# q by tokens for dK: from a scratch tensor in DRAM to replicated copies and transposes inside SBUF

## The chip, the cores and the metric

The kernel runs on one core of one Trainium2 chip. A core has five engines that run independent instruction streams in order and wait for one another on semaphores: TensorE (PE, with weight loads shown apart as PEld), VectorE (DVE), ScalarE (ACT), GpSimd (POOL) and SyncE (SP). Transfers are issued by SP, ACT or POOL and carried out by 16 DMA engines. The metric is the device time of one execution in microseconds; less is better.

## The reference

Two attention blocks stand side by side, and the kernel computes the forward output and all gradients for a given gradient of the output. A is a linear attention; it comes first in time and the change does not touch it. B is an attention with 16 query heads of 28 columns over one shared head of keys and values, for 2048 tokens:

```python
q = (x @ wq).reshape(B, S, H, Dh).transpose(0, 2, 1, 3)   # 16 heads
k = x @ wk                                                # one head
v = x @ wv
scores = einsum("bhqd,bkd->bhqk", q, k) * Dh ** -0.5
p = softmax(scores)
o = einsum("bhqk,bkd->bhqd", p, v)
out = o.transpose(0, 2, 1, 3).reshape(B, S, H * Dh) @ wo
```

For the gradients, with dS the gradient of the scores, dQ is dS times k, and dK is the sum over all heads and queries of dS transposed times q. For dK, q is needed with tokens on the partitions ("q by tokens"), while the scores need it with columns on the partitions (R1, also called qT_B). How q by tokens is made is what changes.

## The kernel before

Block A runs first, then the projections of block B (phase_B_pre): keys, values and q are computed with columns on the partitions; R1 holds four groups g of 128 rows (4 heads of 32 padded columns), 2048 tokens long. q_shift computes a softmax offset for each query and put_shift writes it by small DMAs into row 0 of each head in R1.

The core of block B is one loop over steps u (512 steps and 28 more to drain). A block b of 8 steps is one pair of heads by 256 queries; a step is 256 keys. Eight blocks (64 steps) share a chunk qc of 256 queries. The order of the work is written out by hand (manual_schedule), and the stages are shifted against each other by fixed lags:

- step u: PE makes the scores (rows_SD); ACT turns their two halves into eT by exp (L914, L964).
- w = u - 16: PE makes dP in two banks DB; DVE multiplies the first half with eT into dsT (L925); ACT copies the second half to cp (L927), and POOL multiplies it (L928). dsT has 5 buffers (pool pd_), cp has 3.
- u - 18: DVE transposes dsT in 32 by 32 blocks into dsx (L995), at the end of its step, and so needs both halves.
- u - 20 and u - 19, at even steps: PE sums dQ from dsT (dq_mm).
- u - 27, at odd steps: PE sums dK from dsx and qX (dk_m, L834).
- every fourth step (u % 4 == 3) SP issues a DMA transpose of 32 tiles of 128x128, eT to eN (L966), which dV uses 13 steps later and more (dv_mm). It is the main work of SP's queue.
- once a block POOL also computes prod, don and an R2 entry (o_norm, L808 to L812) and one small product (L817).

Before the change q by tokens comes to qX so. For the first 1024 tokens, phase_B_pre transposes R1 by DMA into qn (L598) and stores it to the DRAM tensor qn_d (L599). For the others, four DMA transposes ahead of the loop fill a second qn (L893), which POOL stores to qn_d in four parts at steps 34 to 58 (L930). POOL then loads each chunk from qn_d in four parts of 32 partitions (L937): at steps 10 to 22 chunk 0, at 66 to 78 chunk 1, and at steps 34, 42, 50 and 58 of each later 64 the next chunk. A buffer qX is [128, 4, 2, 512]: token (b, j, s) stands on partition j of each of four groups of 32 partitions, since the four row groups of the PE each need q. wo, the output weight, is loaded by POOL at step 86, and the softmax offsets of token groups 2 and 3 are put by POOL at step 1.

The DMA issues of POOL are POOL's own instructions: they stand in its stream and take its time. SP's stand in SP's queue[...].

## Time and profile before

| what | before |
|---|---|
| time, median of 3 runs (lowest, highest) | 1080.56 us (1078.34, 1083.28) |
| the profiled execution's own time | 1082.27 us |
| its span, first to last instruction | 1080.6 us |
| busy: PE, DVE, ACT, POOL | 95%, 83%, 81%, 72% |
| TensorE clock, mean over the span | 0.994 |
| first and last exp of the loop (L914) start at | 218.5 and 1003.6 us |
| steps 16 to 34, by the start of their exp | 237.9 to 278.7 us |
| a block of 8 steps later on | 11.96 to 12.17 us for most |

The page of a profile lists the engines' busy time, groups of instructions by line of the kernel with their number and mean time, and a chain: the work that ended last, followed back through what released each step. A trace can also be listed in order of time. "PE agen L661" in a wait is an engine, what it writes and the line; "SPq" is SP's queue. Line numbers are those of the kernel before.

### The profile page before, as it was taken

How to read it: one execution, taken by the hardware profiler on the slowest of the kernel's cores; microseconds unless marked ns; L12 is line 12 of the kernel's file. 1: busy time of each engine (PE TensorE's matmuls, PEld its weight loads, DVE VectorE, ACT ScalarE, POOL GpSimd, SP SyncE). 2: the span in 40 equal slices, each digit the busy share in tenths (PEclk: the TensorE clock that was granted, in tenths of full speed). 3: DMA queues.
4: the chain of work that ended last, by engine and by line, in shares of the span. 5: the costliest groups of instructions: out<-in, count | busy, mean ns of one | idle time of the engine just before them, and what ended most of it. 6: DMA issues, size and time to landing. Idle time of an engine off the chain costs nothing.

```text
span 1080.6 us, 39970 instructions
## 1 busy us (share of the span) xinstructions
PE 1026.0 (95%) x16241; PEld 484.7 (45%) x16241; DVE 898.0 (83%) x1793; ACT 873.2 (81%) x1741; POOL 774.0 (72%) x1018
## 2 busy tenths in 40 slices
PE   9999999996999999999999999999999999999998
PEld 5555545432444444444444444444444444444434
DVE  7887400556999999999999999999999999999933
ACT  6463122585999999999999999999999999999622
POOL 6001242235899888888988988988988898888881
PEclk9999999997999999999999999999999999999999
DMA  9759899199999999999999999999999999999973
GB/s 265 160 110 199 173 204 228 30 185 151 204 208 211 203 202 188 200 180 210 179 185 197 196 195 187 203 181 188 185 209 187 196 198 162 206 187 181 223 133 90
DMA packets 668305, 199.34 MB, mean 184 GB/s; under 512 B 646056, under 2 KB 663760, under 8 KB 668120
## 3 DMA queue, kind: packets, MB, share of 16 engines
q1 hardware_dynamic: 655256, 174.18, 95.7%
q0 software_dynamic: 7904, 18.64, 6.8%
q10 hardware_dynamic: 4960, 3.96, 1.3%
q8 instruction: 127, 2.08, 0.8%
q14 instruction: 58, 0.48, 0.1%
HBM read 20.99 MB, written 12.94 MB: 31 GB/s over the span
## 4 chain that ended last, share of the span: by engine, by line
PE 37%; POOL 21%; ACT 18%; DVE 11%; issue 10%; DMA 4%; ACTq 0%; DVEq 0%; POOLq 0%
POOL dsT L928 16%; PE agen L82 14%; ACT cp L927 9%; ACT eT L964 7%; PE agen L661 7%; PE aacc L82 7%; PE aacc L661 6%; DVE dsx L995 4%; DVE dsT L925 2%; DMA eN<-eT 2%; POOL prod L808 2%; POOL don L811 1%; POOL R L812 1%; ACT eT L914 1%; DMA qX<-qn_d 1%
## 5 line engine op out<-in xcount | busy, mean ns | idle before, releaser
L928 POOL TENSOR_TENSOR dsT<-cp,eT 128x512 bf16<-128x512 bf16 x512 | 587.8, 1156 | 103.7 <-ACT cp L927 97.2
L995 DVE STREAM_TRANSPOSE dsx<-dsT 128x512 f32<-128x512 f32 x512 | 358.0, 699 | 2.8 <-POOL dsT L928 0.3
L925 DVE TENSOR_TENSOR dsT<-agen,eT 128x512 bf16<-128x512 f32 x512 | 342.1, 668 | 20.0 <-PE agen L661 15.2
L661 PEld LDWEIGHTS <-R 32*128 32x128 bf16 (+1 forms) x9104 | 225.3, 94 | 276.1 <-issue 239.5
L914 ACT ACTIVATE eT<-aacc 128x512 bf16<-128x512 f32 x512 | 313.2, 612 | 26.7 <-PE agen L661 15.8
L927 ACT ACTIVATE cp<-agen 128x512 bf16<-128x512 f32 x512 | 315.4, 616 | 12.3 <-PE agen L661 11.2
L964 ACT ACTIVATE eT<-aacc 128x512 bf16<-128x512 f32 x512 | 321.7, 628 | 0.0
L661 PE MATMUL agen<-dsx,qX 32*32 32x512 bf16 x4096 | 269.0, 376 | 3.5 <-DMA qX<-qn_d 3.5
L661 PE MATMUL agen<-doT,R 32*128 32x256 bf16 x2048 | 248.1, 270 | 3.3 <-DVE dsT L925 1.6
L661 PE MATMUL aacc<-R,R 32*128 32x256 bf16 (+1 forms) x2240 | 218.8, 269 | 5.8 <-DVE oTs L804 1.3
L661 PE MATMUL agen<-eT,R 128*32 128x256 bf16 x2048 | 158.2, 275 | 0.1
L661 PE MATMUL agen<-dsT,R 128*32 128x256 bf16 x2048 | 157.3, 275 | 0.1
L661 PEld LDWEIGHTS <-qX 32*32 32x32 bf16 x4096 | 80.1, 89 | 118.4 <-issue 54.6
L661 PE MATMUL aacc<-eN,don 128*32 128x512 bf16 x1024 | 98.1, 383 | 4.3 <-DMA eN<-eT 4.3
L82 PEld LDWEIGHTS <-R 128*128 128x128 bf16 (+1 forms) x517 | 41.0, 99 | 43.9 <-issue 12.3
L407 POOL COPY pk<-R 128x256 bf16<-128x256 bf16 x4 | 1.6, 397 | 73.8 <-DVE R L367 73.7
L82 PE MATMUL agen<-R,R 128*128 128x448 bf16 (+1 forms) x180 | 42.9, 366 | 0.5 <-ACT R L226 0.5
L661 PEld LDWEIGHTS <-don 128*32 128x32 bf16 x1024 | 33.9, 98 | 5.3 <-issue 4.7
L423 DVE TENSOR_TENSOR osb<-aacc,pr 64x448 bf16<-64x448 f32 x2 | 1.2, 617 | 39.1 <-DMA out_dram<-osb 24.9
L825 PE MATMUL aacc<-identB,don 128*32 128x128 bf16 x256 | 18.6, 224 | 14.0 <-POOL don L817 10.2
L949 DVE TENSOR_SCALAR R<-agen 64x256 bf16<-64x256 f32 x64 | 27.3, 427 | 3.6 <-PE agen L661 1.6
L517 ACT ACTIVATE wdq<-agen 128x448 bf16<-128x448 f32 x16 | 8.7, 543 | 24.7 <-PE agen L82 24.7
(232 smaller groups left out, 987.7 us busy)
## 6 DMA issues: line engine op xcount, KB each, us to landing
qX<-qn_d POOLq DMA_DIRECT2D x32, 256.0 KB, 4.4
out_dram<-osb ACTq DMA_DIRECT2D x22, 112.0 KB
eN<-eT SPq DMA_TRANSPOSE x128
xa<-in_A_x_dram SPq DMA_DIRECT2D x8, 224.0 KB
ga<-in_grad_out_dram SPq DMA_DIRECT2D x4, 448.0 KB
xa<-in_grad_out_dram POOLq DMA_DIRECT2D x4, 448.0 KB, 5.8
out_dram<-wdq POOLq DMA_DIRECT2D x8, 224.0 KB, 4.9
eT<-in_grad_out_dram SPq DMA_DIRECT2D x4, 448.0 KB
```

The source lines that it names most:

```text
L82: nc.tensor.matmul(out_ap, lhsT=lhsT, rhs=rhs, start=start, stop=stop, tile_position=(0, 0))
L661: nc.tensor.matmul(out, lhsT=lhsT, rhs=rhs, start=start, stop=stop, tile_position=pos, skip_group_check=True)
L808: nc.gpsimd.tensor_tensor(out=prod[b][:], in0=dnv, in1=os_, op=ALU.mult)
L811: nc.gpsimd.tensor_tensor(out=dn[:], in0=dnv, in1=r_[:].to_broadcast([P, 2, 2, 32]), op=ALU.mult)
L825: nc.tensor.transpose(tp2[q:q + 32, qb * P:(qb + 1) * P], don[b][:, qb, h, :], identB[:, :], tile_position=(0, q))
L914: nc.scalar.activation(out=eT(u)[:, 0, :], in_=sp[0][:, :], func=ACT.Exp, scale=scale)
L925: nc.vector.tensor_tensor(out=dst[:, 0, :], in0=dp[0][:, :], in1=ew[:, 0, :], op=ALU.mult)
L927: nc.scalar.activation(out=cp[:, :], in_=dp[1][:, :], func=ACT.Copy)
L928: nc.gpsimd.tensor_tensor(out=dst[:, 1, :], in0=cp[:, :], in1=ew[:, 1, :], op=ALU.mult)
L949: nc.vector.tensor_scalar(out=qT_B[g][64 * hp:64 * hp + 64, qc * 256:(qc + 1) * 256], in0=oq[64:128, 0:256], scalar1=scale, scalar2=None, ...
L964: nc.scalar.activation(out=eT(u)[:, 1, :], in_=sp[1][:, :], func=ACT.Exp, scale=scale)
L995: nc.vector.transpose(out=dsx[b][:, tp, :, :, :].rearrange("p h t c -> p (h t c)").bitcast(F32), in_=dsT[y][:, :, :].rearrange("p h c -> p ...
```

## The change

The scratch tensor qn_d is gone. For each chunk and group g the columns of R1 are copied inside SBUF into a staging tile, each token repeated four times (qc_copy, two instructions, one per parity s of the token), and one DMA transpose of 8 tiles (qc_T) turns that into the 128 columns g of qX, so that the four partition groups receive their copies at once. Chunk 0 is made ahead of the loop, half of the copies on POOL and half on VectorE, through four of the dsT buffers. The later chunks use one staging tile, qst (a single buffer); POOL copies at steps 30 + 8g and 32 + 8g of each 64, and SP's transpose is issued at step 35 + 8g, behind the eN transpose of the same step. The buffers of even and odd chunks change places. wo is loaded by SP ahead of the loop, and the offsets of token groups 2 and 3 are put by SP at step 11. Everything of PE and ACT stays in its order.

```diff
-            if qc == 1:
-                for g in range(4):
-                    nc.sync.dma_start_transpose(qn[:, :, g * P:(g + 1) * P], qT[:, g, 0:1024])
-                nc.sync.dma_start(qn_d[0:1024, :].rearrange("(t p) c -> p t c", p=P), qn)
...
+        qst = pp_.tile([P, 8, 4, 32], BF16, name="qst", bufs=1)[:, :, :, :]
...
+        def qc_copy(eng, st, qc, g, s):
+            src = qT_B[g][:, qc * 256:(qc + 1) * 256].rearrange("p (b j s) -> p b j s", b=4, s=2)[:, :, :, s]
+            eng.tensor_copy(out=st.rearrange("p (b s) a j -> p b s a j", s=2)[:, :, s, :, :],
+                            in_=src.unsqueeze(2).to_broadcast([P, 4, 4, 32]))
+
+        def qc_T(st, qc, g):
+            nc.sync.dma_start_transpose(qX[qc].rearrange("p b s c -> p (b s) c")[:, :, g * P:(g + 1) * P],
+                                        st.rearrange("p n a j -> p (n a j)"))
...
-            qn = pqa_.tile([P, 8, 512], BF16, name="qX")
+            nc.sync.dma_start(wo, wo_d[:, 0:D].rearrange("(g p) c -> p g c", p=P))
+            qX[0] = pqa_.tile([P, 4, 2, 512], BF16, name="qX")
             for g in range(4):
-                nc.sync.dma_start_transpose(qn[:, :, g * P:(g + 1) * P], R1[:, g, 1024:2048])
+                st = pd_.tile([P, 2, 512], BF16, name="dsT").rearrange("p a (n j) -> p a n j", j=32).rearrange(
+                    "p a (n b) j -> p (a n) b j", b=4)
+                qc_copy(nc.gpsimd, st, 0, g, 0)
+                qc_copy(nc.vector, st, 0, g, 1)
+                qc_T(st, 0, g)
...
-                    for qc in (2, 3):
-                        put_shift(shifts[qc], slice(qc * 512, qc * 512 + 512))
...
+                if u == 11:
+                    for n in (2, 3):
+                        put_shift(nc.sync, shifts[n], slice(n * 512, n * 512 + 512))
...
-                for n in {34: (0,), 42: (1,), 50: (2,), 58: (3,)}.get(u, ()):
-                    nc.gpsimd.dma_start(qn_d[1024 + 256 * n:1280 + 256 * n, :].rearrange("(t p) c -> p t c", p=P),
-                                        qn[:, 2 * n:2 * n + 2, :])
-                for a in {10: (0,), 14: (2,), 18: (1,), 22: (3,), 66: (0,), 70: (2,), 74: (1,), 78: (3,)}.get(u, ()) or {
-                        34: (0,), 42: (2,), 50: (1,), 58: (3,)}.get(u % 64, ()) * (96 < u < 448):
-                    qc = u // 64 + (u > 96)
-                    if a == 0:
-                        qX[qc] = (pqa_ if qc % 2 else pqb_).tile([P, 4, 2, 512], BF16, name="qX")
-                    nc.gpsimd.dma_start(qX[qc][32 * a:32 * a + 32, :, :, :].rearrange("j b s c -> j b (s c)"),
-                                        qn_d[qc * 256:(qc + 1) * 256, :].rearrange("(b j s) c -> j b (s c)", b=4, s=2))
-                if u == 86:
-                    nc.gpsimd.dma_start(wo, wo_d[:, 0:D].rearrange("(g p) c -> p g c", p=P))
+                gq, iq = divmod(u % 64 - 30, 8)
+                qq = u // 64 + 1
+                if 0 <= gq < 4 and u < 448:
+                    if gq == 0 and iq == 0:
+                        qX[qq] = (pqb_ if qq % 2 else pqa_).tile([P, 4, 2, 512], BF16, name="qX")
+                    if iq in (0, 2):
+                        qc_copy(nc.gpsimd, qst, qq, gq, iq // 2)
...
                     if u % 4 == 3:
                         nc.sync.dma_start_transpose(ENs[u // 4 % 6][:, :, :],
                                                     ETs[u // 4 % 5][:, :, :, :].rearrange("p a b c -> p (a b c)"))
+                    if 0 <= gq < 4 and iq == 5 and u < 448:
+                        qc_T(qst, qq, gq)
```

## The prediction

> **What bounds the kernel now.** I read the page first (busy shares, 40 slices), then the windows of the loop, then the timeline of one block, then the chain around the loop's start.

> ```profile
> 360.00:400.00 40.00, 38.35 (x771) 18.02 (x770) 39.08 (x77) 39.65 (x81) 35.77 (x42) 1.00 1.15 202
> 400.00:500.00 100.00, 96.02 (x1873) 44.11 (x1869) 97.32 (x190) 99.00 (x199) 87.87 (x105) 1.00 1.14 191
> ```

> The columns are the stretch, its length, then busy PE, PEld, DVE, ACT, POOL, the clock, the DMA share and GB/s. In the loop ACT is busy 99%, DVE 97%, PE 96%, POOL 88%: three engines in lockstep with next to no slack, so a late result at any of them moves the end. POOL's place in one block, with SP's queue (step 107, which is 43 of its 64):

> ```profile
> 391.17 0.60 ACT L964 ACTIVATE eT<-aacc 128x512 bf16<-128x512 f32 x1
> 391.80 5.89 SPq L966 DMA_TRANSPOSE eN<-eT  x1
> 394.88 2.27 POOL L928 TENSOR_TENSOR dsT<-cp,eT 128x512 bf16<-128x512 bf16 x2
> 397.46 1.16 POOL L928 TENSOR_TENSOR dsT<-cp,eT 128x512 bf16<-128x512 bf16 x1 [0.31 <-ACT cp L927]
> 400.21 0.69 DVE L995 STREAM_TRANSPOSE dsx<-dsT 128x512 f32<-128x512 f32 x1
> ```

> ACT ends step 107 at t = 391.77 and SP starts the eN transpose at once. POOL ends the dsT of step 110 at 397.15 (t + 5.4), that of 111 at 398.62 (t + 6.85), and DVE's dsx of step 113, which reads the latter, starts at 400.21 (t + 8.4). So POOL leads its reader by 1.6 us. Over the loop that is the same within 0.2 us. SP's queue:

> ```profile
> L966 SPq DMA_TRANSPOSE eN<-eT x128: 4760/5421/12268, 226.6 to 1005.2; - x128
> ```

> 5.4 us (median) of each 6.08 us (4 steps) go to eN. Third, the start of the loop, in the chain of waits:

> ```profile
> 232.62 16.89 DMA eN<-eT
> ...
> 255.79 10.60 DMA qX<-qn_d
> 266.44 1.88 PE agen L661 x7
> ```

> Here the loop waits for two transfers: PE stands idle from 245.2 for 4.35 us and from 262.9 for 3.5 us, and each time the granted clock is at 0.5 for 6.8 us.

> [...] the 8-tile transposes of L598, alone on the queue, reach their semaphore 2.0 to 2.2 us after SP has issued them; eN, of 1 MB, 3.3 us after (median, 1.3 to 5.3). [...] in the trace an eN takes 5.8 us in the blocks where POOL loads qX and about 5.2 elsewhere. [...]

> **The change part by part.**

> *Copies on POOL.* From 397 and 561 ns: 0.85 ns an element, 0.62 us for 512. The source steps 4 bytes and repeats, which no row shows; bounds 0.55 and 0.95 us. Two a block in four of eight blocks, 1.24 us, in place of one DMA issue of 0.58 us. POOL's block is 8 x 1.14 + 1.3 = 10.4 us when back to back, 11.7 with copies, of 12.0 to 12.2: it fits. Blocks with a qX issue last 12.16 us, those without 11.96 to 12.04; I take copy for issue as 0 (bounds -0.15 to +0.3 us in 28 blocks, -4 to +8). What covers them is POOL's idle time before dsT, 0.3 us a step; without it each copy would cost its length.

> *Transposes on SP.* 8 tiles took 1.23 to 1.39 us at L598 and L893. Four in 64 steps add 5.4 us to 16 x 5.2 = 83 of 97: the queue still fits, with eN's 13 steps of lead as cover.

> *The new wait.* qst is one buffer. The first copy of group g + 1 stands at step 38 + 8g and has to wait until the transpose of group g, issued at step 35 + 8g, has landed. That transpose is behind the eN of the same step. From t, ACT's end of step 35: 0.03 until eN starts, 5.3 for eN, 0.06, 1.3 for the transpose, 2.7 until it lands (between the 2.0 of a lone one and the 3.3 of eN, behind whose data it runs): t + 9.4. POOL is at the copy at t + 5.4 and waits 4.0 us. Behind the copy stands dsT of step 39: 9.4 + 0.62 + 1.16 = t + 11.2, but DVE wants it at t + 8.4. DVE is 2.8 us late; behind its dsx stands L925 of the next step, and PE waits for that to free the DB bank before the scores that ACT needs. ACT has at most some 0.4 us in hand (PE's scores of 383.72 to 384.0 are used at 384.14), so 2.4 us are lost. Since t moves with the delay and POOL gains only some 0.4 us a block, the next copy meets the same wait. Three waits per chunk (g = 1, 2, 3; for g = 0 the last transpose is 34 steps old) in 7 chunks: 21 x 2.4 = 50 us. Bounds for one: eN 4.9, landing 2.0, slack 0.8: 1.2 us; eN 5.9, landing 3.6, copy 0.95, no slack and 0.5 more for prod (L808), which is pushed behind the copies and waited for by DVE: 5.0 us.

> *The entry.* L598, L599, L893 and the four loads of chunk 0 go: SP's first eN was at 226.6, the second landed at 249.5. Now SP's order is wo, four 8-tile transposes (copies from 218.2 on POOL, 218.7 on DVE; 4 x 0.62 us, and 4 x 0.3 to 0.7 on DVE, hidden in its gap of 2.06 us at 218.7), eN at about 224.7, 230.0, then the eight puts[...], then eN from 239.5 every 5.3 us. Needed by dV at steps 20, 28, 36 (244, 256, 268): landed at 238.6, 253, 264. qX of chunk 0 is there by 228, wanted at 263. Both waits go. Steps 16 to 34 took 278.65 - 237.86 = 40.8 us; undisturbed steps took 1.62 us up to 26 (while PE also makes do_nat) and 1.52 after: 28.4. Gain 12.4 us (bounds 5, if eN stays at 6 us and dV waits again, and 14).

> *The first chunk* meets an SP queue that is still late: the eighth eN ends at about 271 while step 35 is at 268.2, so the first wait is 3 us longer: +3.

> *wo and the puts off POOL*: 0.8 us at step 86, and 4.5 us at 222 to 233, where POOL was idle but for prod of block 0, 2.3 us late: 0 (gain at most 1).

> Sum on the profile's span: 1080.6 + 50.4 + 3 - 12.4 + 0 = 1121.6. The profiled execution took 1082.3, the median of the runs is 1080.56, so on it the same 41 us give 1122.

> **The rivals.**

> *The stall is mostly absorbed.* The landing is early (t + 8.4) and the engines give 0.8 us or more: 0.5 to 1.2 us a wait, 10 to 25 us, against 9 gained: 1083 to 1097. For it: eN can take 4.76 us, and it loses the traffic of the qX loads. Against: ACT's 99%.

> *Not slower: the landing comes in time.* One mechanism: without the loads from DRAM the queue drains so fast that the transposes land before POOL's copy matters. Price: the 12.4 us of the entry alone, 1068. It decides where a wait costs less than 9.4 / 21 = 0.45 us, that is at a landing before t + 7.4. Against: eN's shortest issue, 4.76, with 1.3 and the 2.0 of the earliest landing is already t + 8.1, at which DVE is 1.5 us late.

> *The clock falls.* [...] it runs 6.8 us at half clock, as twice at the entry: some 2 to 3 us more each, 1165 (1150 to 1190). Against: PE gets work between the pieces (dq_mm, dv_mm, first scores).

> *The entry doesn't do what it should*: eN stays slow (9 to 12 us) for another reason than the q traffic, and the 12 us don't come: 1134. It lies in the range of the likeliest.

> **How the numbers follow.** The stall at near full size 0.68 (1104 to 1145, entry lost included); the clock too 0.12; mostly absorbed 0.13, of which 0.03 within 0.5%; in time 0.07, of which 0.06 faster. 0.5% (5.4 us) is about what a measurement of this kernel can tell from no change. So faster 0.06, same 0.04, slower 0.90. The range 1092 to 1152 leaves out the fast end (0.07 and a third of the absorbed) and most of the clock case.

> **What would show it.** Right: POOL's copy line with idle time before it released by "DMA qX<-qst", about 4 us each at 21 places, some 85 us in all; DVE's dsx waiting for POOL dsT; ACT's share in the loop down to 93% or so, blocks of some 14.5 us in threes, others at 12.0; no wait for eN or qX before 280 us and a clock of 1.00 there. Wrong: a landing within 7.4 us of t, a tolerance of DVE or ACT above 1.5 us, or clock at 0.5 inside the loop.

## The result, and the profile after

The changed kernel takes 1135.92 us (median of 4 runs, 1133.29 to 1137.67) against 1081.58 (4 runs beside it, 1078.34 to 1083.28): a ratio of 1.0504, interval 1.0468 to 1.0540. Predicted were 1122, in a range of 1092 to 1152. Its profiled execution took 1134.53 us, with a span of 1132.8.

The windows of the loop, in the columns of the prediction's table (stretch, length, busy PE, PEld, DVE, ACT, POOL, clock, DMA share, GB/s):

```profile
360.00:400.00 40.00, 35.91 (x664) 15.95 (x658) 34.32 (x67) 34.41 (x70) 31.95 (x39) 0.91 0.96 166
400.00:500.00 100.00, 89.57 (x1732) 41.39 (x1729) 90.00 (x175) 91.84 (x184) 81.23 (x97) 0.99 1.06 180
```

ACT was busy 99% here; now it is 86% and 92%. All engines lost share together: they wait, and no one is the new bound. On the page the slices of the clock and two groups of instructions say where:

```profile
PEclk9999999999899999989998999999899989999999
...
L1003 DVE STREAM_TRANSPOSE dsx<-dsT 128x512 f32<-128x512 f32 x512 | 358.4, 700 | 47.1 <-POOL dsT L939 44.6
...
L832 POOL COPY qst<-R 128x512 bf16<-128x512 bf16 x56 | 34.1, 610 | 74.0 <-DMA qX<-qst 64.7
```

After the bar stands the idle time of the engine ahead of such instructions and what ended most of it. POOL stood 74.0 us ahead of its copies, nearly all for the transpose of q; DVE stood 47.1 us ahead of dsx for POOL's dsT. The clock has slices below full speed all along the loop. The kernel before had its only one at the loop's start, and hardly a wait at dsx:

```profile
PEclk9999999997999999999999999999999999999999
...
L995 DVE STREAM_TRANSPOSE dsx<-dsT 128x512 f32<-128x512 f32 x512 | 358.0, 699 | 2.8 <-POOL dsT L928 0.3
```

One stalled block in the timeline (start, length, engine, line; in brackets the idle time before and its releaser). Step 99, which is 35 of its 64, ends on ACT at t = 380.09:

```profile
380.12 5.41 SPq L972 DMA_TRANSPOSE eN<-eT  x1
384.20 1.15 POOL L939 TENSOR_TENSOR dsT<-cp,eT 128x512 bf16<-128x512 bf16 x1 [0.31 <-ACT cp L938]
385.58 1.30 SPq L836 DMA_TRANSPOSE qX<-qst  x1
390.17 0.61 POOL L832 COPY qst<-R 128x512 bf16<-128x512 bf16 x1 [4.82 <-DMA qX<-qst]
390.74 2.27 POOL L939 TENSOR_TENSOR dsT<-cp,eT 128x512 bf16<-128x512 bf16 x2
391.92 0.60 ACT L938 ACTIVATE cp<-agen 128x512 bf16<-128x512 f32 x1 [2.41 <-POOL dsT L939]
391.92 0.71 DVE L1003 STREAM_TRANSPOSE dsx<-dsT 128x512 f32<-128x512 f32 x1 [3.43 <-POOL dsT L939]
393.33 0.29 DVE L800 TENSOR_TENSOR oTs<-aacc,rl 128x128 f32<-128x128 f32 x1
393.67 0.40 PE L656 MATMUL aacc<-R,R 32*128 32x256 bf16 x2 [0.72 <-DVE oTs L800]
394.29 0.60 ACT L924 ACTIVATE eT<-aacc 128x512 bf16<-128x512 f32 x1 [1.29 <-PE agen L656]
395.26 0.60 ACT L970 ACTIVATE eT<-aacc 128x512 bf16<-128x512 f32 x1
```

The short transpose of q stands behind the long eN, and SP starts it at t + 5.5. It lands (the last step of its semaphore in the trace) at 390.12 (t + 10.0), and 0.05 us later POOL starts the copy for which it has stood idle since t + 5.3. From there the block runs down a chain with no slack in it: copy, dsT, dsx on DVE, the next product on DVE, rl and oTs (they norm the output and read a bank of the scores), PE's scores, ACT's exps, whose last ends at 395.86, 5.69 us after the copy began. ACT stands idle twice on the way: 2.41 us at step 42 of the chunk, for dsT, and 1.29 us at step 43, for scores that PE could not write before DVE had made oTs. The view of the tile qst sums the cause:

```profile
L832 POOL COPY qst<-R x56: 602/609/615, 263.8 to 950.8; 128x512 bf16<-128x512 bf16 x56
L836 SPq DMA_TRANSPOSE qX<-qst x28: 1249/1320/2143, 278.7 to 959.1; - x28
its engine sat idle before it (us, times) until:
  DMA qX<-qst: 64.7, 18
```

With the three waits that this view puts down to a DVE instruction that ended at about the same time, it is 21 waits with 74.0 us: three in each of seven chunks, 1.6 to 6.3 us each.

At the entry the long waits for transfers are gone from the chain. Around the loop's start it now holds only instructions, and the first piece over 1.2 us is POOL's first wait:

```profile
238.47 0.92 PE agen L656 x10
...
263.49 0.59 ACT cp L938
...
275.88 6.27 issue
```

Where the time went, by two stretches of the two traces: from the start of step 16 to that of step 34, 29.3 us in place of 40.8 (11.5 less); from ACT's end of step 35 to its end of step 511 ("the loop" from here on), 787.6 in place of 723.3 (64.3 more). The two make the 52 us between the spans, the rest 0.5 less.

### The profile page after: what moved, and what is told of

Same layout as the page of the kernel before. It is cut to its first block, busy times and chain, and to the rows that moved or that the text cites. A ratio compares the mean times of both kernels' runs of the same rounds, so it can differ in the third digit from the quotient of the medians.

```text
span 1132.8 us, 40036 instructions
## 1 busy us (share of the span) xinstructions
PE 1046.4 (92%) x16241; PEld 490.0 (43%) x16241; DVE 905.4 (80%) x1797; ACT 874.9 (77%) x1741; POOL 781.0 (69%) x1033
## 4 chain that ended last, share of the span: by engine, by line
PE 43%; ACT 24%; issue 15%; POOL 10%; DVE 6%; DMA 1%; ACTq 0%; DVEq 0%; POOLq 0%
PE agen L81 14%; ACT cp L938 12%; PE agen L656 11%; ACT eT L970 9%; PE aacc L656 9%; POOL dsT L939 9%; PE aacc L81 7%; DVE dsT L936 2%; DVE dsx L1003 1%; PE aacc L821 1%; ACT eT L924 1%; PE aacc L790 1%; POOL qst L832 1%; DMA dsx<-R 1%; DVE oTs L800 0%
## 5 line engine op out<-in xcount | busy, mean ns | idle before, releaser
L1003 DVE STREAM_TRANSPOSE dsx<-dsT 128x512 f32<-128x512 f32 x512 | 358.4, 700 | 47.1 <-POOL dsT L939 44.6
L656 PEld LDWEIGHTS <-R 32*128 32x128 bf16 (+1 forms) x9104 | 226.6, 95 | 329.3 <-issue 293.3
L656 PE MATMUL agen<-dsx,qX 32*32 32x512 bf16 x4096 | 278.3, 387 | 0.0
L656 PE MATMUL agen<-doT,R 32*128 32x256 bf16 x2048 | 251.6, 275 | 3.1 <-DVE dsT L936 1.4
L656 PE MATMUL aacc<-R,R 32*128 32x256 bf16 (+1 forms) x2240 | 222.2, 274 | 27.6 <-DVE oTs L800 22.5
L656 PE MATMUL agen<-dsT,R 128*32 128x256 bf16 x2048 | 165.7, 280 | 20.0 <-POOL dsT L939 19.8
L656 PE MATMUL agen<-eT,R 128*32 128x256 bf16 x2048 | 164.9, 280 | 0.1
L656 PE MATMUL aacc<-eN,don 128*32 128x512 bf16 x1024 | 101.9, 395 | 0.0
L832 POOL COPY qst<-R 128x512 bf16<-128x512 bf16 x56 | 34.1, 610 | 74.0 <-DMA qX<-qst 64.7
L81 PEld LDWEIGHTS <-R 128*128 128x128 bf16 (+1 forms) x517 | 40.8, 98 | 43.9 <-issue 12.0
L804 POOL TENSOR_TENSOR prod<-R,oTs 128x128 f32<-128x128 bf16 x64 | 27.5, 430 | 9.3 <-DVE oTs L800 9.3
L422 DVE TENSOR_TENSOR osb<-aacc,pr 64x448 bf16<-64x448 f32 x2 | 1.2, 617 | 37.8 <-ACT wdq L516 23.9
```

What stands on the lines that cost most here:

```text
L81: nc.tensor.matmul(out_ap, lhsT=lhsT, rhs=rhs, start=start, stop=stop, tile_position=(0, 0))
L656: nc.tensor.matmul(out, lhsT=lhsT, rhs=rhs, start=start, stop=stop, tile_position=pos, skip_group_check=True)
L804: nc.gpsimd.tensor_tensor(out=prod[b][:], in0=dnv, in1=os_, op=ALU.mult)
L832: eng.tensor_copy(out=st.rearrange("p (b s) a j -> p b s a j", s=2)[:, :, s, :, :], in_=src.unsqueeze(2).to_broadcast([P, 4, 4, 32]))
L1003: nc.vector.transpose(out=dsx[b][:, tp, :, :, :].rearrange("p h t c -> p (h t c)").bitcast(F32), in_=dsT[y][:, :, :].rearrange("p h c -> p ...
```

## The experiments

Medians in us, ratio to the kernel before on the same chip with its interval, and the loop from each run's trace. The runs lie on several chips, and the kernel before spreads by some 15 us on two of them, so a few microseconds between medians of different chips say nothing by themselves:

| run | time | ratio | loop |
|---|---|---|---|
| before | 1081.6 | 1 | 723.3 |
| after | 1135.9 | 1.0504 (1.0468 to 1.0540) | 787.6 |
| q's transpose ahead of eN | 1066.3 | 0.9847 (0.9814 to 0.9879) | 723.3 |
| no q made in the loop | 1063.7 | 0.9826 (0.9797 to 0.9855) | 716.8 |
| copies two steps later | 1101.5 | 1.0183 (1.0143 to 1.0223) | 754.2 |
| copies one step later | 1109.7 | 1.0250 (1.0216 to 1.0284) | 761.1 |
| both: ahead, and two steps later | 1069.8 | 0.9921 (0.9890 to 0.9953) | 723.1 |
| ahead, puts and wo back on POOL | 1065.8 | 0.9893 (0.9855 to 0.9931) | 717.7 |
| ahead, entry of before | 1075.7 | 0.9939 (0.9912 to 0.9966) | 722.4 |
| work for PE in the stall | 1136.9 | 1.0516 (1.0459 to 1.0573) | 787.7 |
| q's transpose between halves of eN | 1082.6 | 1.0012 (0.9992 to 1.0032) | 733.8 |

**The landing alone.** My theory: the stall comes from where the transpose of q stands in SP's queue. The rival: from the new work and traffic as such.

```diff
-                    if u % 4 == 3:
-                        nc.sync.dma_start_transpose(ENs[...], ETs[...])
                     if 0 <= gq < 4 and iq == 5 and u < 448:
                         qc_T(qst, qq, gq)
+                    if u % 4 == 3:
+                        nc.sync.dma_start_transpose(ENs[...], ETs[...])
```

> The changed kernel with one move: at step 35 + 8g the 8-tile transpose of q is issued ahead of the eN transpose of the same step, not behind it. Theory 'landing' (POOL's copy waits for the transpose behind eN to land): it now lands some 3.6 us after ACT's end of the step, POOL comes to the copy at 5.4 us, no wait is left, no half clock in the loop: 1070 us (1064 to 1076). Rival 'traffic' (28 more transposes on SP's queue and 56 more copies on POOL are themselves what the loop can't bear): nothing of that is less, so 1115 us or more.

1066.33 us (1066.05 to 1069.08), 1.5% faster than the kernel before, with the same instructions as the changed kernel in a different order on one queue. A block of it in the timeline (t = 574.86) and the group of its page:

```profile
574.59 1.37 SPq L836 DMA_TRANSPOSE qX<-qst  x1
576.06 10.95 SPq L974 DMA_TRANSPOSE eN<-eT  x2
...
580.03 0.63 POOL L832 COPY qst<-R 128x512 bf16<-128x512 bf16 x1
```

```profile
L832 POOL COPY qst<-R 128x512 bf16<-128x512 bf16 x56 | 34.3, 613 | 6.5 <-DMA qX<-qst 5.7
```

The transpose lands at 579.45 (t + 4.6), before POOL comes to the copy at t + 5.2. POOL's idle time at the copies went from 74.0 to 6.5 us. The whole loss was a matter of some five microseconds of landing: t + 4.9 in the mean over the 21 places, t + 9.5 before.

**What copies and transposes cost when nobody waits.**

```diff
-        qst = pp_.tile([P, 8, 4, 32], BF16, name="qst", bufs=1)[:, :, :, :]
...
-                    if gq == 0 and iq == 0:
-                        qX[qq] = (pqb_ if qq % 2 else pqa_).tile([P, 4, 2, 512], BF16, name="qX")
-                    if iq in (0, 2):
-                        qc_copy(nc.gpsimd, qst, qq, gq, iq // 2)
+                    qX[qq] = qX[0]
...
-                    if 0 <= gq < 4 and iq == 5 and u < 448:
-                        qc_T(qst, qq, gq)
```

> Leaves out the making of q for chunks 1 to 7: every chunk uses the qX of chunk 0 (dK is then another quantity), no copy and no transpose of q in the loop. The entry is that of the changed kernel. All theories: the floor, the kernel before less the 11 us of the entry and less what the 28 loads of q cost it in POOL's stream (about 0.15 us a block): 1066 us (1062 to 1071). Theory 'landing' says that the two runs above with moved copies or transposes come within 6 us of it; 'traffic' says that they stay 40 us or more above it.

1063.71 us. So 56 copies on POOL (34 us of its busy time) and 28 transposes on SP (37 us of its queue) cost 2.6 us beside the order above. This is the floor for where q is made inside the loop.

**Late POOL in place of early landing.** If a wait ends earlier relative to POOL, it does not matter which of the two moves: so I thought.

```diff
-                    if iq in (0, 2):
-                        qc_copy(nc.gpsimd, qst, qq, gq, iq // 2)
+                    if iq in (2, 4):
+                        qc_copy(nc.gpsimd, qst, qq, gq, iq // 4)
```

> The changed kernel with the two copies of a group two steps later (32 + 8g and 34 + 8g), the transpose where it was, behind eN. Theory 'landing': POOL comes to the copy 8.3 us after ACT's end of step 35, the landing is at 9.4 to 9.6, so POOL still idles 1 to 1.5 us at 21 places, but its next dsT is ready at about 11.3 us and DVE wants it at 11.5: nothing lost, 1071 us (1065 to 1080). Rival 'traffic': as the changed kernel, 1115 us or more. A third view, that any wait of POOL costs its length, gives 25 us: 1095.

and one step later only (`iq in (1, 3)`):

> The same with the copies one step later than in the changed kernel (31 + 8g and 33 + 8g). Theory 'landing': POOL comes at 6.9 us and waits 2.6 us; the dsT behind the copy is ready at 11.3 us, DVE wants it at 9.95, so DVE is 1.3 us late and 0.9 to 1.3 us are lost at 21 places: 1070 + 19 to 27, about 1092 us (1083 to 1100), with hardly any half clock. Rival 'traffic': 1115 us or more. If most of the loss of the changed kernel is the half clock and not the wait, it is nearer 1075.

1101.53 and 1109.71 us: both missed, too slow. POOL's waits did shrink, to 24.7 and 43.2 us over the same 21 places, but the loop lost 30.9 and 37.8 us: here each microsecond of waiting cost about one, and what is left of the wait is not tolerated at all. The timeline of the first of the two shows the path (t = 378.4, landing t + 10.2):

```profile
388.59 0.61 POOL L832 COPY qst<-R 128x512 bf16<-128x512 bf16 x1 [1.91 <-DMA qX<-qst]
...
391.37 0.61 POOL L832 COPY qst<-R 128x512 bf16<-128x512 bf16 x1
...
395.54 0.29 PE L821 MATMUL aacc<-identB,don 128*32 128x128 bf16 x2 [1.19 <-POOL don L813]
...
397.78 0.60 ACT L924 ACTIVATE eT<-aacc 128x512 bf16<-128x512 f32 x1 [1.95 <-PE agen L656]
```

The late copies push prod and don (L804 to L813), and PE waits for don ahead of scores that ACT needs: at that step of the block ACT stood idle 18.8 us for PE in this trace, 2.0 us in that of before. The other part of the 30.9 us was not followed up. The row of don had no margin from the start. Its group on the page of before, and then on that of this run:

```profile
L825 PE MATMUL aacc<-identB,don 128*32 128x128 bf16 x256 | 18.6, 224 | 14.0 <-POOL don L817 10.2
```

```profile
L821 PE MATMUL aacc<-identB,don 128*32 128x128 bf16 x256 | 18.7, 225 | 24.5 <-POOL don L813 20.0
```

In before, PE takes don 0.05 us after it has ended in most of the blocks that load qX, having waited 0.2 to 0.5 us for it. I had measured POOL's margin at the reader dsx and taken it for POOL's margin.

**The place, or the wait in it?** The two misses could also mean that copies cost time at the later place in any case.

> The transpose of q ahead of the step's eN (as in the run that gave 1066.3) and the copies two steps later, at steps 32 and 34 of each group, where they stand right ahead of prod and don (L804, L807). Theory A: late copies lost time only because the landing made POOL wait; POOL is at the copy at t + 8.3, the transpose lands before t + 6.5, nothing waits, and the 28 groups last 12.0 to 12.15 us: 1068 (1064 to 1073). Theory B: the place itself costs, since 1.2 us of copies ahead of don go straight through to PE, which waits for don (in the kernel before don ends 0.05 us before PE takes it): every group lasts 12.6 us or more with no wait at any copy, 1085 to 1100.

The edit is the first and the third together. 1069.79 us (1068.46 to 1073.7), a loop of 723.1, and no wait at any of the 56 copies:

```profile
L832 POOL COPY qst<-R 128x512 bf16<-128x512 bf16 x56 | 34.2, 611 | 0.0
```

Of the 28 blocks with copies most last 12.13 us, ten 12.3 to 12.7, 12.25 in the mean against 12.06 in the run further down with the puts on POOL. So the place does cost, 0.2 us a block, but the 31 us were the wait.

**Is a stalled block the landing plus a constant?** From the trace of after: over the 21 stalled blocks the landing is at t + 9.47 (mean; 8.0 to 11.5), the copy starts 0.05 us later, and the block ends 5.58 us after that (5.49 to 5.70 in every one). Undisturbed, in the run with the transpose ahead, those last steps take 6.84 us from a copy at t + 5.19: the chain behind the copy gives 1.1 to 1.3 us and then nothing. So a landing moved to t + 6.9 should leave waits that still cost.

```diff
+                        isT = 0 <= gq < 4 and iq == 5 and u < 448
+                        for k in range(2) if isT else (0,):
+                            n = 2 if isT else 4
+                            nc.sync.dma_start_transpose(
+                                ENs[u // 4 % 6][:, 16 * k:16 * k + 8 * n, :],
+                                ETs[u // 4 % 5][:, 2 * k:2 * k + n, :, :].rearrange("p a b c -> p (a b c)"))
+                            if isT and k == 0:
+                                qc_T(qst, qq, gq)
```

> The changed kernel, but at the steps with a transpose of q the eN is issued in two halves of 16 tiles, with the transpose of q between them. From 2.7 us for a half (of 4.9 to 5.5 for the whole), 1.3 for the transpose and 2.8 until it lands: landing at t + 6.9 in place of t + 9.5, so POOL, at the copy at t + 5.2, waits some 1.7 us, 35 us in all. Cycle theory (from the traces of after: a stalled block is landing + 0.05 + 5.5 us, with 1.34 us of give in the whole chain from copy to block end and no more): blocks of 12.45 in place of 12.03, 21 x 0.42 = 9, 3 more in the first chunk, on 1066.3 of the run without waits: 1078 (1073 to 1084), no half clock. The give of my prediction (1.6 us at DVE with ACT's 0.4, so that dsT of step 39 at t + 8.7 is late for nothing): the waits are there but cost nothing outside the first chunk, 1069 (1066 to 1071).

1082.57 us, the time of the kernel before; the loop lost 10.5 us on 723.3 and the median 16 on 1066.33, where the constant said 12 and the margins of my prediction 3. The landing came at t + 6.63 in the mean. A block of the timeline (t = 790.17):

```profile
792.85 1.98 SPq L836 DMA_TRANSPOSE qX<-qst  x1
...
797.47 0.61 POOL L832 COPY qst<-R 128x512 bf16<-128x512 bf16 x1 [1.83 <-DMA qX<-qst]
...
802.36 0.60 ACT L970 ACTIVATE eT<-aacc 128x512 bf16<-128x512 f32 x1
```

From the copy at t + 7.29 to the end of the block at 802.96 it is again 5.5 us, so 12.79 in place of 12.03. The rule holds only so far: a copy at t + 6.51 cost nothing (a block of 12.04), as it says, but two blocks that followed a late one lasted 13.2 us with copies at t + 6.35. What a late block leaves behind is not in it.

**The clock.** In the trace of after PE's clock is at 0.5 in 12 stretches of 3.41 or 6.83 us inside the loop, 61.4 us in all. ACT's idle time by step of the block, added up over the trace: 49.6 us at steps 42 and 43 of the chunk and their like (the stall), and 14.2 us at the two steps behind them, up to 0.82 us at a time and only in blocks in which the clock was at 0.5 or had just been. Those 14 us looked like the price of the clock.

```diff
+                    if u < 448 and u % 64 in (42, 50, 58):
+                        for _ in range(12):
+                            mmt(oq[0:32, 256:512], vaug[:, 0, :], eT(u - 2)[:, 0, 0:256], (0, 0), True, True)
                     o_dq((u - 2, u - 1), (u - 20, u - 19))
```

> The changed kernel with work for PE put into its stall: at steps 42, 50 and 58 of each of the 7 chunks, ahead of dq_mm, 12 more matmuls of 128 by 32 by 256 into the unused half of oq (some 1.3 us; the results are read by nobody). In the changed kernel ACT idles 14.2 us in all at the two steps after a stall (steps 4 and 5 of 8), only where the granted clock is at 0.5 there, and 49.6 us at steps 2 and 3, in the stall itself. If those 14 us are the price of the clock[...]: few half-clock stretches are left in the loop, ACT's idle time at steps 4 and 5 goes to below 4 us, and the time goes from 1135.9 to 1124 (1118 to 1130), POOL's waits at the copy staying at 60 us or more. If the 14 us come from something else that the late copies hold up, or if the filler is not covered by the stall: 1134 or more.

The page of this run:

```profile
PEclk9999999999899999999999999999999999999999
...
L832 POOL COPY qst<-R 128x512 bf16<-128x512 bf16 x56 | 34.3, 613 | 80.8 <-DMA qX<-qst 73.2
```

One half-clock stretch of the 12 is left, ACT's idle time at those two steps fell from 14.2 to 1.3 us, and the time did not move: 1136.94 us. The time came back elsewhere: 7.0 us more at steps 42 and 43, 6.9 more where PE waits for don. POOL, which came sooner to its next copy, waited 6.8 us longer there. In both runs a stalled block ends 5.58 us after its copy (mean of 21), so its length is set by the landing. The slow clock lay inside the next wait, and was free.

**The entry.** Two runs undo parts of it, both with the transpose ahead in the loop. First the puts and wo only:

```diff
-            nc.sync.dma_start(wo, wo_d[:, 0:D].rearrange("(g p) c -> p g c", p=P))
...
                 if u == 1:
...
+                    for n in (2, 3):
+                        put_shift(nc.gpsimd, shifts[n], slice(n * 512, n * 512 + 512))
...
-                if u == 11:
-                    for n in (2, 3):
-                        put_shift(nc.sync, shifts[n], slice(n * 512, n * 512 + 512))
...
+                if u == 86:
+                    nc.gpsimd.dma_start(wo, wo_d[:, 0:D].rearrange("(g p) c -> p g c", p=P))
```

> The same kernel with the transpose ahead, but the eight puts back on POOL at step 1 and the load of wo back on POOL at step 86, as in the kernel before. My prediction priced these two moves at 0, gain at most 1 us: 1066 (1064 to 1068). Rival: the puts on SP at step 11 hold the third eN back by 4.6 us, so taking them off SP gains 2 to 4 us at the entry (1062 to 1064); or on POOL they delay the first prod and don, which stand on no margin: 1068 to 1071.

1065.75 us; the median with them on SP was 1066.33, on another chip. By the ratios, 0.9893 and 0.9847, POOL would be the worse place by 5 us, but their intervals overlap: no difference is shown. Then, on top of that, q for chunk 0 through DRAM as in before (L598, L599, L893 and the first four loads of before put back, the copies and transposes ahead of the loop taken out):

> Loop as in the kernel with the transpose ahead, entry as in the kernel before: q by tokens through DRAM for chunk 0 (L598, L599, L893 and the four loads at steps 10 to 22 of the kernel before), puts and wo on POOL. If the entry part is worth what the trace of after shows there (steps 16 to 34 took 29.3 us in place of 40.8): 1066.3 + 11.5 = 1078 (1075 to 1080), with two half-clock stretches before 280 us, and the loop's part of the gain is 1081 - 1078 = 3 to 4 us, from 28 blocks of 12.03 in place of 12.16 us. If the two parts are not independent (eN stays late into the loop and the first transposes of q with it): above 1082.

1075.68 us, in a wide spread (1063.93 to 1081.37 over 20 runs), and both waits for transfers are back in the chain:

```profile
232.33 15.71 DMA eN<-eT
...
254.31 8.61 DMA qX<-qn_d
```

So the way of q at the entry is worth 9.9 us by the medians and 5 by the two ratios. In this profiled execution steps 16 to 34 took 35.7 us against 29.3, with one of the two half-clock stretches that were expected before 280 us (granted clock 0.995 in the mean, 0.998 with the entry of the change); in that of before, where the clock was at 0.5 for 6.83 us from the middle of each of the two waits on, 40.8.

A second staging tile, the obvious cure, was not run. That the wait comes of the single buffer is therefore read from the program and the traces; no run with two shows it.

## Why the prediction was right, and where it was off

**Right: the wait, its place and its count.** POOL's first copy of a group waits for the landing of the group before, 21 times; 74.0 us in all against 84 or so. The landing was put at t + 9.4 and came at 9.37 (mean without the first chunk's first). A copy took 0.610 us for 0.62, a transpose 1.32 for 1.3. That the queue's order made it is shown by the run with the order turned round (6.5 us of waits at the copies, 1066.33 us). The gap that comes again and again is ACT's at steps 42 and 43, 49.6 us in all, and the buffer behind it is qst.

**Right: the entry.** 11.5 us in the trace against 12.4, with SP's queue as forecast (the second, fourth and sixth eN landed at 237.7, 255.0 and 265.4; forecast were 238.6, 253 and 264). The times of the runs put it at 5 to 10 us; with the entry of before they spread from 1063.93 to 1081.37. Copies in place of DMA issues, put at 0, gave 0.13 us in each of 28 blocks (12.03 for 12.16, medians with the transpose ahead and before), within the bounds; wo and the puts, put at 0, can't be told from 0.

**Off: the loss per wait.** Predicted 2.4 us, 50.4 with 3 more for the first chunk; the 21 blocks lost 21 x (15.11 - 12.03) = 64.7. The step that is off is "dsT of step 39 at t + 11.2, but DVE wants it at t + 8.4", with ACT's 0.4 us as the rest of the margin, and the path behind it. It let a block end 5.05 us after the landing (12.05 + 2.4 - 9.4). Measured are 0.05 + 5.58, so 0.58 us more, 12 us over 21 waits, which is the difference of 11.3 but for roundings. I priced one stop, on a path from DVE's dsx over the DB bank and PE's scores to ACT. The trace shows two, and neither is that one. At step 42 POOL itself stops ACT: cp has three buffers, so the cp of step 42 takes the one that the dsT of step 39 reads. In the block shown it starts 0.03 us after that dsT has ended, 2.5 us after the last thing of PE it waits for; this is 25.0 us, at 16 of the 21 waits. At step 43 PE stops ACT: behind dsx in DVE's stream stand rl and oTs, which read a bank that PE's next scores need; this is 1.0 to 1.3 us at 19 of the 21. The whole chain back to ACT gives 1.1 to 1.3 us, not 1.6, and POOL does not get its lead back from one wait to the next: it came to the copy at t + 6.0 in the mean, not 5.4. That 2.4 us came within a quarter of the measured 3.1 by a path that was not taken is in part luck.

Two terms are missing or slipped. The block after the third wait of a chunk had no price; it lasts 12.9 us in the mean against 12.1 in the run with the transpose ahead and the puts on POOL, some 6 us over seven chunks. And the lower bound of one wait, from its own terms 8.3 + 0.62 + 1.16 - 8.4 - 0.8, is 0.9 us and not 1.2. Two readings were too broad, without effect on the result: of the four transposes of L893 only the first took 1.23 us, the others 1.57 to 2.29; and the 2.0 us from the end of an issue to its landing rest on the 2.0 to 2.2 us of L598 alone.

The missed runs with later copies come from the same habit: a margin read at one reader (dsx) was used at a place where another reader (PE, of don) has none.

**The rivals.** "In time" needed a landing before t + 7.4 and was priced at 1068: in the changed kernel it lands 2 us too late, and with the transpose ahead the kernel takes 1066. That border was too kind as well: between the halves of eN it landed at t + 6.6 in the mean, and the loop still lost 10.5 us. "Mostly absorbed" falls: there is 1.1 to 1.3 us of give in each block, already used up. "The entry doesn't come" falls. "The clock falls" came, at 12 of 21 waits, against my reason that PE has work between the pieces; but its price of 2 to 3 us each was wrong, it is nothing that could be measured: with 12 half-clock stretches and with one the kernel takes 1135.92 and 1136.94 us (medians), and a stalled block ends 5.58 us after its copy in both.

What stays open: the 5.6 us between the loops of the runs with puts on SP (723.3) and on POOL (717.7), both with the transpose ahead. The profiled execution of the former took 1069.08 us, its other three 1066.05 to 1066.35, so up to 2.7 us of the 5.6 may be that one execution's. The trace of the former has one half-clock stretch (404 us, with blocks of 13.7 and 13.3 us) and six short waits at copies (6.5 us), that of the latter no such stretch (granted clock 0.998 and 1.000 in the mean), 1.2 us of waits at copies, and no block of them over 12.34; whether the place of the puts makes the rest was not tested.

## What to carry to other kernels

A single buffer between a copy and a transfer is a loop through the queue of that transfer: price the landing by all that stands ahead of it on the issuing queue (here t + 9.5 us behind eN, t + 4.9 ahead of it), and where a short transfer feeds a wait and a long one does not, issue the short one first. To price a late producer follow every reader behind it back to the engine that is never idle, since the smallest margin on those paths counts and not that of the first reader (here 0.05 us at don, 1.6 us at dsx). While a wait on something else is longer than a slowdown, curing the slowdown gains nothing (here 12.9 us less idle time of ACT behind the stalls, and 1136.94 us for 1135.92): look at what the wait takes back.

## What the runs showed of the hardware

In the loop of after a DMA transpose of 8 tiles took 1.3 us of SP's queue in the median (1.25 to 2.14), and over the whole trace one of 32 tiles took 4.8 to 6.2; the landing of the short one came 1.9 to 2.0 us after its issue had ended in the first three at the entry, which no eN preceded, and 1.8 to 3.8 us after it behind an eN in the loop. POOL's copy with a source step of 4 bytes and a fourfold repeat took 609 ns there in the median (602 to 615) for 512 elements; its plain copies of before took 397 ns for 256 (L407) and 561 for 448 (L490), a line that puts 512 at 616.
